# Second row tile's sums by GpSimd's addition, tail inputs third on SyncE's queue, swapped half by copies

## The chip, the cores and the metric

The kernel runs on one core of a Trainium2 chip. The metric is the device time of one execution in microseconds; the time before is the median of three runs. The profile is of one more execution, taken by the hardware profiler; its span runs from the first to the last instruction, and the execution's own time is a little longer than its span.

Engines in the profile: PE is TensorE's matmuls, PEld its weight loads, DVE is VectorE, ACT is ScalarE, POOL is GpSimd, SP is SyncE, which here only issues DMAs. ACTq, SPq and POOLq are the engines' queues.

## The reference

A cross network of six layers on 4096 rows of 416 columns:

```python
B, F, D, L = 4096, 26, 16, 6          # Din = 416
def reference(x0, ws, bs):            # [4096, 416], [6, 416, 416], [6, 416], bf16
    x = x0
    for l in range(ws.shape[0]):
        x = x0 * (x @ ws[l] + bs[l]) + x
    return x
```

Since every layer adds a multiple of x0, x after layer l is x0 * (1 + S_l), where S_l is the sum of all products and biases so far. The kernel keeps S in PSUM, lets TensorE add each layer's product to it, and multiplies by x0 on the way out.

## The kernel before

**Tiling.** The 4096 rows are four blocks of 1024 (s = 0 to 3), each worked through all six layers (l = 0 to 5) before the next. A block is held transposed: features on the partitions, rows on the free axis. The 416 features are three chunks of 128 (c, or m as output and k as input) and a tail of 32. A block has two halves of 512 rows (h). The sum of half h, chunk c lies in PSUM bank 3h+c; banks 6 and 7 (`T_BANK`) hold the tails' sums.

**A layer** has, in this order on TensorE: the main matmuls of the first half (`main`, four 32-column matmuls side by side for each pair of chunks), the tails' contribution to all six banks (`tail_rows`), the tails' own sums (`tail_outs`), and the main matmuls of the second half. As soon as a bank is complete, VectorE adds the bias and multiplies by x0 in one operation of 128x512 (`leave`, L455, or L442 in the last layer but one of the last block): this is the next layer's x. The tail's sum leaves by ScalarE (L465) and GpSimd (L478). The tail exists twice, as it is and with neighbouring groups of 32 partitions swapped; from layer 1 on the swapped half comes from copies of ScalarE and GpSimd (`swap`, L430, L432).

**The head** (s = 0, l = 0). The first 512 rows (`xin_sb`) come in row layout and are transposed by TensorE (L542) and copied by VectorE (L552); the next 512 come by a transposing DMA. `tail_in` (L402) brings the first block's tails into their layout: 16 narrow matmuls against the identity, eight for the straight half into bank 4 and eight for the swapped half into bank 5, copied out by ScalarE (L416) and VectorE (L420). It needs `xtl_sb`, the tail inputs of rows 512 to 1023, which is the third load on ScalarE's queue (L241). In the order of TensorE it stands after the main matmuls of k=1, together with the bias sums, whose result VectorE copies to `cb_sb` (L575).

**The ending** (s = 3). The last layer is computed in row layout, eight row tiles of 128 rows (j = 0 to 7), so that its result goes straight to the output. Row tile j's result gathers in bank `ROW_BANKS[j]` = (6, 7, 0, 1, 2, 3, 4, 5)[j]. The old sums S still lie transposed in banks 0 to 5, so `keep_sum` copies them with the last bias to `sS_sb` (five copies on ScalarE, L488, one on VectorE, L490), and `row_sums` turns them with the identity into the row tiles' banks. TensorE's order: the narrow main matmuls of rows 0 to 3 (`row_main`), the tails of all eight rows (`row_tails`, two groups: rows 0, 2, 4, 6, then rows 1, 3, 5, 7), the sums of rows 1 to 3, then for each of the rows 4 to 7 its main matmuls and sums. VectorE multiplies each finished row by x0 (`finish`, L718), and the row is stored.

Row 0 is treated apart: it has no `row_sums`. Its share of the old sums comes through a transposing DMA of the last layer's x (`transpose_first`, L493, into `xl_sb`), to which GpSimd adds x0 times the last bias (L621, L636). ScalarE copies row 0's new product out of PSUM (L725), GpSimd multiplies (L729) and adds (L733).

**Order.** Each engine runs its instructions in the order in which the code adds them. A small planner (`Plan.add`) works out the waits from keys that each operation reads and writes. For PSUM banks its rule is stricter than for other keys, a reader also waits for the earlier readers on other engines:

```python
            if key[0] == "ps":
                needs += [(r, False) for r in self.readers.get(key, ())]
```

Of the kernel before, what the change touches and what calls it, by code (L numbers as in the profile page):

```python
# [6 lines left out]
FP32 = mybir.dt.float32  # L7
# [111 lines left out]
def bass_standalone__dcn_v2_cross__recsys_kernel(  # L119
# [8 lines left out]
    NC = 3  # L128
# [7 lines left out]
    JS = SB // 128  # L136
    NJ = B // 128
    T_BANK = (6, 7)
    HALVES = range(2)
    CH = range(NC)  # L140

    with ExitStack() as es:

        def sb(name, shape, dt=BF16):
            return es.enter_context(nc.sbuf_tensor(name, shape, dt))
# [15 lines left out]
        f32_sb = sb("f32_sb", [128, D], FP32)  # L161
        xl_sb = sb("xl_sb", [128, DF])
        bl_sb = sb("bl_sb", [128, DF])
        y_sb = sb("y_sb", [128, 2, D], FP32)
        p_sb = sb("p_sb", [128, D], FP32)
        xo_sb = sb("xo_sb", [128, NS - 1, NC, SB])
# [20 lines left out]
        def quad(q):  # L187
            return slice(32 * q, 32 * q + 32)
# [48 lines left out]
        load("scalar", wt_sb[quad(0), 0, :], ws[0, DF:D, :], "wt0", [("wtq",)])  # L237
        for k in CH:
            queue = "sync" if k else "scalar"
            load(queue, w_sb[:, 0, k, :], ws[0, 128 * k:128 * k + 128, :], "w0_%d" % k, [("w", 0, k)])  # L240
        load("scalar", xtl_sb[:, 4:JS, :], x0_v[:, 4:JS, DF:D], "xtl0", [("xtl", 0)])  # L241
        load_transposed(0, H, SB)
# [32 lines left out]
        P.add("gpsimd", lambda e: e.memset(wc_sb[:, :, :], 0.0), writes=[("wc", "wt%d" % i) for i in range(3)])  # L275
        P.add("gpsimd", lambda e: e.memset(y_sb[:, 1, DF:D], 0.0), writes=[("yz",)])

# [123 lines left out]

        def tail_in():  # L402
            def fn(pe):
                for o in range(2):
                    for r in range(2):
                        for g in range(4):
                            j = 2 * (g ^ o) + r
                            src = xin_sb[:, j, DF:D] if j < 4 else xtl_sb[:, j, :]
                            ins = mm(
                                pe, ps[quad(g), TAIL_BANKS[o], r * 128:(r + 1) * 128], src, ident[:, :], r == 0, (0, 32 * g),  # L410
                            )
                return ins

            P.add("tensor", fn, reads=[("ident",), ("xtl", 0), ("xin", 0), ("xin", 1)], adds=[("ps", b) for b in TAIL_BANKS])
            P.add(
                "scalar", lambda e: e.activation(out=x0t_sb[:, 0, 0, :], in_=ps[:, TAIL_BANKS[0], 0:G], func=ACTF.Copy),  # L416
                reads=[("ps", TAIL_BANKS[0])], writes=[("x0t", 0)],
            )
            P.add(
                "vector", lambda e: e.tensor_copy(out=x0t_sb[:, 0, 1, :], in_=ps[:, TAIL_BANKS[1], 0:G]),  # L420
                reads=[("ps", TAIL_BANKS[1])], writes=[("x0t", 0, "swapped")],
            )

        def swap(tile, key, engines):
            for g, eng in enumerate(engines):
                if eng is None:
                    continue
                dst, src = tile[quad(g), 1, :], tile[quad(g ^ 1), 0, :]
                if eng == "scalar":
                    fn = lambda e, d=dst, s=src: e.activation(out=d, in_=s, func=ACTF.Copy)  # L430
                else:
                    fn = lambda e, d=dst, s=src: e.tensor_copy(out=d, in_=s)  # L432
                P.add(eng, fn, reads=[key], parts=[key + ("swapped",)], shifts=True)


# [47 lines left out]

        def keep_sum(h, c, eng):
            lo = 0 if h else 128
            o, i, b = sS_sb[:, c, h * H + lo:(h + 1) * H], ps[:, bank(h, c), lo:H], cb_sb[:, c, L - 1:L]
            if eng == "scalar":
                fn = lambda e: e.activation(out=o, in_=i, func=ACTF.Identity, bias=b)  # L488
            else:
                fn = lambda e: e.tensor_scalar_add(o, i, b)  # L490
            P.add(eng, fn, reads=[("ps", bank(h, c)), ("cb",)], writes=[("sS", c, h)])

        def transpose_first():  # L493
            P.add(
                "sync", lambda e: e.dma_start_transpose(
                    xl_sb.rearrange("p (c f) -> p c f", c=NC), xj[:, 0, :, :].rearrange("p c f -> p (c f)")
                ), reads=[("xT", (L - 1) % 2, c, 0) for c in CH], writes=[("xl",)], dma="xl",
            )
# [34 lines left out]
        B_BANK = 7  # L533
        TAIL_BANKS = (4, 5)

# [47 lines left out]
        for s in range(NS):  # L583
            for l in range(L):
# [3 lines left out]
                if s == 0 and l == 0:  # L588
                    for k in CH:
                        for part in range(2) if k == 0 else (None,):  # L590
                            for m in CH:
                                main(s, l, 0, m, k, part)
                        if k == 1:
                            tail_in()
                            bias_sums()
# [4 lines left out]
                else:  # L600
# [6 lines left out]
                    if ending:  # L607
                        transpose_first()
                    tail_outs(s, l, False)
# [7 lines left out]
                if s > 0 and l == (3 if s < NS - 1 else 2):  # L617
                    store_block(s - 1)
                if s == NS - 1 and l == 3:
                    P.add(  # L620
                        "gpsimd", lambda e: e.tensor_tensor(  # L621
                            out=y_sb[:, 0, 0:DF], in0=xr_sb[:, 0, 0:DF], in1=bl_sb[:, :], op=ALU.mult
                        ), reads=[("xr",), ("bl",)], writes=[("z",)],
                    )
                if ending:
# [8 lines left out]
                    )  # L634
                    P.add(
                        "gpsimd", lambda e: e.tensor_tensor(  # L636
                            out=y_sb[:, 1, 0:DF], in0=y_sb[:, 0, 0:DF], in1=xl_sb[:, :], op=ALU.add
                        ), reads=[("z",), ("xl",)], writes=[("y",)],
                    )
                    for c in CH:  # L640
                        keep_sum(0, c, "scalar")
                for m in CH:
# [3 lines left out]
                if ending:  # L646
                    for c in CH:
                        keep_sum(1, c, ("scalar", "scalar", "vector")[c])
            if s < NS - 1:
# [4 lines left out]
            if s == NS - 2:  # L654
                load("sync", xr_sb[:, :, :], x0_v[:, (NS - 1) * JS:NJ, :], "xr", [("xr",)])
                load("sync", bl_sb[:, :], bs[L - 1:L, 0:DF].to_broadcast([128, DF]), "bl", [("bl",)])

# [56 lines left out]
        def finish(j):  # L714
            b, jj = ROW_BANKS[j], (NS - 1) * JS + j
            if j:
                P.add(
                    "vector", lambda e: e.tensor_tensor(  # L718
                        out=o_sb[:, jj, :], in0=ps[:, b, 0:D], in1=xr_sb[:, j, :], op=ALU.mult
                    ), reads=[("ps", b), ("xr",)], writes=[("ol", j)],  # L720
                )
                return
            t, p, o = f32_sb[:, :], p_sb[:, :], o_sb[:, jj, :]
            P.add(
                "scalar", lambda e: e.activation(out=t, in_=ps[:, b, 0:D], func=ACTF.Copy),  # L725
                reads=[("ps", b)], writes=[("f32",)],
            )
            P.add(
                "gpsimd", lambda e: e.tensor_tensor(out=p, in0=t, in1=xr_sb[:, j, :], op=ALU.mult),  # L729
                reads=[("f32",), ("xr",)], writes=[("p",)],  # L730
            )
            P.add(
                "gpsimd", lambda e: e.tensor_tensor(out=o, in0=p, in1=y_sb[:, 1, :], op=ALU.add),  # L733
                reads=[("p",), ("y",), ("yz",)], writes=[("ol", j)],
            )

        def store_rows(queue, a, b):
            ja = (NS - 1) * JS
            P.add(
                queue, lambda e: e.dma_start(out_v[:, ja + a:ja + b, :], o_sb[:, ja + a:ja + b, :]),  # L740
                reads=[("ol", j) for j in range(a, b)], writes=[("outl", a)], dma="outl",
            )
# [3 lines left out]
        row_tails()  # L746
        finish(0)
        for j in range(1, 4):
            row_sums(j, False)
            finish(j)  # L750
        for j in range(4, 8):
# [3 lines left out]
        P.add("sync", None, reads=[("out", s) for s in range(NS - 1)])  # L755
        STORES = (
            ("scalar", 1, 3), ("scalar", 3, 4), ("sync", 4, 5), ("scalar", 0, 1), ("sync", 5, 6), ("scalar", 6, 7),
            ("sync", 7, 8),
        )
        for queue, a, b in STORES:  # L760
            store_rows(queue, a, b)
        P.add("sync", None, reads=[("outl", a) for _, a, _ in STORES])

# [29 lines left out]
```

## Time and profile before

| what | value |
|---|---|
| median of 3 runs | 127.68 us (127.36 to 127.82) |
| the profiled execution's own time | 128.1 us |
| its span | 126.8 us |
| granted TensorE clock | 1.00 |
| PE busy | 123.6 us, 97% |
| DVE busy | 100.0 us, 79% |
| ACT busy | 43.0 us, 34% |
| POOL busy | 41.0 us, 32% |

By stretches of the span, busy microseconds of each engine:

| stretch, us | PE | DVE | ACT | POOL |
|---|---|---|---|---|
| 0 to 8.7, head | 7.85 | 2.79 | 2.42 | 3.92 |
| 8.7 to 115.4, layers | 106.70 | 88.85 | 36.40 | 32.33 |
| 115.4 to 118.3 | 2.90 | 2.37 | 1.67 | 0.68 |
| 118.3 to 121.0, narrow rows and row tails | 2.70 | 2.33 | 2.00 | 1.66 |
| 121.0 to 125.1, row tiles | 3.47 | 3.67 | 0.47 | 2.37 |
| 125.1 to 126.8, last store | 0 | 0 | 0 | 0 |

A line of the timeline gives the start, the time from the first start to the last end of the group, the engine, the line of the kernel, the operation, what it writes and reads with shapes, the count, and in brackets the engine's idle time before it with what ended it. Groups on PE all bear the line of the helper `mm` (L295); they are told apart by their tiles. Instructions of one engine overlap a little: six of 0.74 us in a row take 4.04 us.

### The profile page before, as it was taken

The numbers are of one execution on the slowest core, as the hardware profiler recorded it, in microseconds if no ns is written. First come the engines' busy times: TensorE is split into PE (matmuls) and PEld (weight loads), VectorE is DVE, ScalarE is ACT, GpSimd is POOL, SyncE is SP. The second block draws the span as 40 slices with busy tenths as digits, with TensorE's granted clock in tenths as the row PEclk, the third lists the DMA queues.
The fourth block names the chain that finished last, engine by engine and source line by source line (L and its number), as shares of the span: only waits on it lengthen the run. The fifth ranks groups of instructions, "written<-read, shape, count | busy, mean of one in ns | idle before, by whom it ended". The sixth has DMA issues, their size and how long they took to land.

```text
span 126.8 us, 5226 instructions
## 1 busy us (share of the span) xinstructions
PE 123.6 (97%) x2373; PEld 64.6 (51%) x2373; DVE 100.0 (79%) x157; ACT 43.0 (34%) x94; POOL 41.0 (32%) x84
## 2 busy tenths in 40 slices
PE   7999999999999999999999999999999999999992
PEld 5654555555545545545545545555555455455561
DVE  2449779779779779788798797797797797797974
ACT  3324225225205225234213242252222252252910
POOL 6505324134014044053122142251320440543590
DMA  3995999010039596107019695107007990070107
GB/s 108 254 253 157 308 158 158 25 25 0 8 83 130 115 213 70 36 16 274 0 32 207 115 163 99 31 16 252 22 0 173 108 292 5 14 255 10 31 20 249
DMA packets 35013, 14.21 MB, mean 112 GB/s; under 512 B 26186, under 2 KB 34992, under 8 KB 34992
## 3 DMA queue, kind: packets, MB, share of 16 engines
q1 hardware_dynamic: 33536, 13.19, 48.4%
q10 hardware_dynamic: 1424, 0.70, 1.9%
q8 instruction: 18, 0.29, 1.0%
q14 instruction: 3, 0.02, 0.1%
q0 software_dynamic: 32, 0.01, 0.0%
HBM read 3.89 MB, written 3.41 MB: 58 GB/s over the span
## 4 chain that ended last, share of the span: by engine, by line
PE 97%; DVE 0%; issue 0%
PE ps L295 94%; PE ps L303 2%; PE ps L542 1%; DVE o_sb L718 0%
## 5 line engine op out<-in xcount | busy, mean ns | idle before, releaser
L455 DVE SCALAR_TENSOR_TENSOR xT_sb<-ps,cb_sb,x0T_sb 128x512 bf16<-128x512 f32 x114 | 76.8, 743 | 15.6 <-PE ps L295 15.6
L295 PE MATMUL ps<-xT_sb,w_sb 128*32 128x512 bf16 (+1 forms) x1596 | 84.2, 364 | 0.0
L295 PEld LDWEIGHTS ps<-xT_sb,w_sb 128*32 128x32 bf16 x1596 | 40.9, 97 | 37.2 <-issue 4.0
L465 ACT ACTIVATE t_sb<-ps,cb_sb 64x256 f32<-64x256 f32 x46 | 21.6, 470 | 57.2 <-PE ps L295 56.9
L478 POOL TENSOR_TENSOR xt_sb<-t_sb,x0t_sb 128x256 bf16<-128x256 f32 x20 | 13.4, 672 | 66.6 <-ACT t_sb L465 66.6
L430 ACT ACTIVATE xt_sb<-xt_sb 32x256 bf16<-32x256 bf16 x38 | 15.7, 414 | 15.1 <-POOL xt_sb L478 14.9
L295 PE MATMUL ps<-x0T_sb,w_sb 128*32 128x512 bf16 (+1 forms) x348 | 19.2, 369 | 0.0
L432 POOL COPY xt_sb<-xt_sb 32x256 bf16<-32x256 bf16 x38 | 14.9, 393 | 2.4
L455 DVE SCALAR_TENSOR_TENSOR xo_sb<-ps,cb_sb,x0T_sb 128x512 bf16<-128x512 f32 x18 | 12.1, 743 | 2.5 <-PE ps L295 2.5
L295 PEld LDWEIGHTS ps<-x0T_sb,w_sb 128*32 128x32 bf16 x348 | 9.1, 101 | 7.7 <-issue 1.1
L295 PE MATMUL ps<-xt_sb,wt_sb 32*128 32x512 bf16 (+1 forms) x152 | 11.6, 326 | 0.0
L295 PE MATMUL ps<-xt_sb,wc_sb 32*128 32x256 bf16 x76 | 7.3, 268 | 0.0
L295 PEld LDWEIGHTS ps<-xt_sb,wt_sb 32*128 32x128 bf16 x152 | 2.3, 91 | 8.1 <-DVE xT_sb L455 8.1
L478 POOL TENSOR_TENSOR xot_sb<-t_sb,x0t_sb 128x256 bf16<-128x256 f32 x3 | 2.0, 672 | 9.9 <-ACT t_sb L465 9.9
L295 PE MATMUL ps<-w_sb,xT_sb 128*32 128x416 bf16 (+1 forms) x60 | 5.0, 339 | 0.0
L442 DVE SCALAR_TENSOR_TENSOR xT_sb<-ps,cb_sb,x0T_sb 128x512 bf16<-128x512 f32 x6 | 4.0, 744 | 0.8 <-PE ps L295 0.8
L718 DVE TENSOR_TENSOR o_sb<-ps,xr_sb 128x416 bf16<-128x416 f32 x7 | 3.7, 583 | 0.8 <-PE ps L295 0.8
L295 PEld LDWEIGHTS ps<-xt_sb,wc_sb 32*128 32x128 bf16 x76 | 3.9, 93 | 0.2
L303 PE MATMUL ps<-const-bfloat16-1.0 128*128 128x256 bf16 x12 | 2.7, 417 | 0.8 <-PEq L778 0.8
L552 DVE COPY x0T_sb<-ps 128x256 bf16<-128x256 bf16 x6 | 1.4, 292 | 2.2 <-PE ps L542 2.2
L295 PEld LDWEIGHTS ps<-w_sb,xT_sb 128*32 128x32 bf16 (+1 forms) x60 | 2.3, 97 | 1.2
L488 ACT ACTIVATE sS_sb<-ps,cb_sb 128x384 bf16<-128x384 f32 (+1 forms) x5 | 2.7, 629 | 0.0
(48 smaller groups left out, 32.3 us busy)
## 6 DMA issues: line engine op xcount, KB each, us to landing
out_dram<-o_sb SPq DMA_DIRECT2D x2, 832.0 KB, 4.8
w_sb<-in_ws_dram SPq DMA_DIRECT2D x5, 312.0 KB, 3.9
out_dram<-o_sb SPq DMA_DIRECT2D x2, 416.0 KB, 3.2
xr_sb<-in_x_dram SPq DMA_DIRECT2D x1, 832.0 KB, 5.0
xin_sb<-in_x_dram SPq DMA_DIRECT2D x2, 208.0 KB, 2.8
wt_sb<-in_ws_dram SPq DMA_DIRECT2D x4, 104.0 KB, 3.3
out_dram<-o_sb ACTq DMA_DIRECT2D x3, 104.0 KB, 1.9
out_dram<-o_sb SPq DMA_DIRECT2D x3, 104.0 KB, 1.7
```

Source lines behind the costliest of these rows:

```text
L295: return pe.matmul(dst, lhsT=lhsT, rhs=rhs, start=start, stop=True, skip_group_check=True, tile_position=pos,)
L303: ins = pe.matmul(ps[:, 7, 0:256], lhsT=const[:, 0:128], rhs=const, start=True, stop=True)
L430: fn = lambda e, d=dst, s=src: e.activation(out=d, in_=s, func=ACTF.Copy)
L432: fn = lambda e, d=dst, s=src: e.tensor_copy(out=d, in_=s)
L442: "vector", lambda e: e.scalar_tensor_tensor(out=xj[:, js, c, :], in0=ps[:, bank(h, c), :].rearrange("p (j f) -> p j f", f=128), scalar=cb ...
L455: "vector", lambda e: e.scalar_tensor_tensor(out=dst, in0=ps[:, bank(h, c), :], scalar=cb_sb[:, c, l:l + 1], in1=x0T_sb[:, c, o:o + H], op ...
L465: "scalar", lambda e, p=p, h=h: e.activation(out=dst[p, :], in_=ps[p, T_BANK[h], 0:G], func=ACTF.Identity, bias=cb_sb[p, NC, l:l + 1]), re ...
L478: "gpsimd", lambda e: e.tensor_tensor(out=dst, in0=t, in1=x0t_sb[:, s, 0, :], op=ALU.mult),
L488: fn = lambda e: e.activation(out=o, in_=i, func=ACTF.Identity, bias=b)
L542: ins = pe.transpose(out=psT[:, b, j * 128:(j + 1) * 128], in_=xin_sb[:, 2 * i + j, c * 128:(c + 1) * 128], identity=ident[:, :],)
L552: "vector", lambda e, d=dst, s=src: e.tensor_copy(out=d, in_=s),
L718: "vector", lambda e: e.tensor_tensor(out=o_sb[:, jj, :], in0=ps[:, b, 0:D], in1=xr_sb[:, j, :], op=ALU.mult), reads=[("ps", b), ("xr",)], ...
```

## The change

Three parts.

*The head.* `xtl_sb` becomes the third load on SyncE's queue; the first layer's weights of k=2 move to ScalarE's queue, and those of k=1 become the fourth load on SyncE's. `tail_in` makes the straight half alone (eight matmuls, bank 5) and stands after the main matmuls of k=0; the swapped half comes from `swap` with VectorE, GpSimd, VectorE and ScalarE.

*The old sums of rows 0 and 1* (JX = 2). VectorE computes (S + last bias) * x0 for 256 rows in the transposed layout (`first_rows_next`, three operations behind the leaves of the first half), and one transposing DMA brings both row tiles to `y_sb` in row layout. Row 1 so loses its `row_sums`, as row 0 had none. The load of the last bias, GpSimd's product and sum with it, and a memset are gone. `keep_sum` leaves out 256 rows in place of 128 in the first half, and all six copies are on ScalarE.

*Finishing.* Row 0's product is split: VectorE the first 128 columns, ScalarE and GpSimd the other 288. Row 1's product is all VectorE's. GpSimd adds y to both (384 columns), ScalarE copies the 32 tail columns of both, and every row has a store of its own.

```diff
-        for k in CH:
-            queue = "sync" if k else "scalar"
+        load("sync", xtl_sb[:, 4:JS, :], x0_v[:, 4:JS, DF:D], "xtl0", [("xtl", 0)])
+        for k, queue in ((0, "scalar"), (2, "scalar"), (1, "sync")):
             load(queue, w_sb[:, 0, k, :], ws[0, 128 * k:128 * k + 128, :], "w0_%d" % k, [("w", 0, k)])
-        load("scalar", xtl_sb[:, 4:JS, :], x0_v[:, 4:JS, DF:D], "xtl0", [("xtl", 0)])
...
+        def tail_in():
+            def fn(pe):
+                for r in range(2):
+                    for g in range(4):
+                        j = 2 * g + r
+                        src = xin_sb[:, j, DF:D] if j < 4 else xtl_sb[:, j, :]
+                        ins = mm(
+                            pe, ps[quad(g), TAIL_BANK, r * 128:(r + 1) * 128], src, ident[:, :], r == 0, (0, 32 * g),
+                        )
+                return ins
+
+            P.add("tensor", fn, reads=[("ident",), ("xtl", 0), ("xin", 0), ("xin", 1)], adds=[("ps", TAIL_BANK)])
+            P.add(
+                "scalar", lambda e: e.activation(out=x0t_sb[:, 0, 0, :], in_=ps[:, TAIL_BANK, 0:G], func=ACTF.Copy),
+                reads=[("ps", TAIL_BANK)], writes=[("x0t", 0)],
+            )
+            swap(x0t_sb[:, 0], ("x0t", 0), ("vector", "gpsimd", "vector", "scalar"))
...
-        def keep_sum(h, c, eng):
-            lo = 0 if h else 128
+        def keep_sum(h, c):
+            lo = 0 if h else JX * 128
             o, i, b = sS_sb[:, c, h * H + lo:(h + 1) * H], ps[:, bank(h, c), lo:H], cb_sb[:, c, L - 1:L]
-            if eng == "scalar":
-                fn = lambda e: e.activation(out=o, in_=i, func=ACTF.Identity, bias=b)
-            else:
-                fn = lambda e: e.tensor_scalar_add(o, i, b)
-            P.add(eng, fn, reads=[("ps", bank(h, c)), ("cb",)], writes=[("sS", c, h)])
-
-        def transpose_first():
+            P.add(
+                "scalar", lambda e: e.activation(out=o, in_=i, func=ACTF.Identity, bias=b),
+                reads=[("ps", bank(h, c)), ("cb",)], writes=[("sS", c, h)],
+            )
+
+        def first_rows_next():
+            o = (NS - 1) * SB
+            for c in CH:
+                P.add(
+                    "vector", lambda e, c=c: e.scalar_tensor_tensor(
+                        out=yT_sb[:, :, c, :], in0=ps[:, bank(0, c), 0:JX * 128].rearrange("p (j f) -> p j f", f=128),
+                        scalar=cb_sb[:, c, L - 1:L],
+                        in1=x0T_sb[:, c, o:o + JX * 128].rearrange("p (j f) -> p j f", f=128),
+                        op0=ALU.add, op1=ALU.mult,
+                    ), reads=[("ps", bank(0, c)), ("cb",), ("x0T", NS - 1, c, 0)], writes=[("yT", c)],
+                )
             P.add(
                 "sync", lambda e: e.dma_start_transpose(
-                    xl_sb.rearrange("p (c f) -> p c f", c=NC), xj[:, 0, :, :].rearrange("p c f -> p (c f)")
-                ), reads=[("xT", (L - 1) % 2, c, 0) for c in CH], writes=[("xl",)], dma="xl",
+                    y_sb.rearrange("p j (c f) -> p (j c) f", f=128), yT_sb.rearrange("p j c f -> p (j c f)")
+                ), reads=[("yT", c) for c in CH], writes=[("y",)], dma="y",
             )
...
                                 main(s, l, 0, m, k, part)
+                        if k == 0:
+                            tail_in()
                         if k == 1:
-                            tail_in()
                             bias_sums()
...
                     if ending:
-                        transpose_first()
+                        first_rows_next()
...
-                        keep_sum(0, c, "scalar")
+                        keep_sum(0, c)
...
-                        keep_sum(1, c, ("scalar", "scalar", "vector")[c])
+                        keep_sum(1, c)
...
+            p, y, hi = p_sb[:, j, :], y_sb[:, j, 0:DF], D if j else 128
+            P.add(
+                "vector", lambda e: e.tensor_tensor(out=p[:, 0:hi], in0=ps[:, b, 0:hi], in1=xr[:, 0:hi], op=ALU.mult),
+                reads=[("ps", b), ("xr",)], writes=[("p", j, "vector")],
+            )
+            if hi < D:
+                P.add(
+                    "scalar", lambda e: e.activation(out=f32_sb[:, hi:D], in_=ps[:, b, hi:D], func=ACTF.Copy),
+                    reads=[("ps", b)], writes=[("f32",)],
+                )
+                P.add(
+                    "gpsimd", lambda e: e.tensor_tensor(out=p[:, hi:D], in0=f32_sb[:, hi:D], in1=xr[:, hi:D], op=ALU.mult),
+                    reads=[("f32",), ("xr",)], writes=[("p", j, "gpsimd")],
+                )
+            P.add(
+                "gpsimd", lambda e: e.tensor_tensor(out=o[:, 0:DF], in0=p[:, 0:DF], in1=y, op=ALU.add),
+                reads=[("p", j, "vector"), ("p", j, "gpsimd"), ("y",)], writes=[("ol", j)],
+            )
...
         row_tails()
-        finish(0)
-        for j in range(1, 4):
+        for j in range(JX):
+            finish(j)
+        for j in reversed(range(JX)):
+            finish_tail(j)
+        for j in range(JX, 4):
             row_sums(j, False)
             finish(j)
...
-        STORES = (
-            ("scalar", 1, 3), ("scalar", 3, 4), ("sync", 4, 5), ("scalar", 0, 1), ("sync", 5, 6), ("scalar", 6, 7),
-            ("sync", 7, 8),
-        )
...
+        for queue, j in (
+            ("scalar", 2), ("sync", 3), ("scalar", 0), ("sync", 4), ("scalar", 5), ("sync", 6), ("scalar", 1), ("sync", 7),
+        ):
+            store_row(queue, j)
```

More of the change, by code (lines that the diff above doesn't have):

```diff
@@ L137, in bass_standalone__dcn_v2_cross__recsys_kernel @@
     NJ = B // 128
+    JX = 2
     T_BANK = (6, 7)
@@ L161, in bass_standalone__dcn_v2_cross__recsys_kernel @@
         f32_sb = sb("f32_sb", [128, D], FP32)
[L162 to L165, printed above, removed]
+        yT_sb = sb("yT_sb", [128, JX, NC, 128])
+        y_sb = sb("y_sb", [128, JX, DF])
+        p_sb = sb("p_sb", [128, JX, D], FP32)
         xo_sb = sb("xo_sb", [128, NS - 1, NC, SB])
@@ L275, in bass_standalone__dcn_v2_cross__recsys_kernel @@
         P.add("gpsimd", lambda e: e.memset(wc_sb[:, :, :], 0.0), writes=[("wc", "wt%d" % i) for i in range(3)])
-        P.add("gpsimd", lambda e: e.memset(y_sb[:, 1, DF:D], 0.0), writes=[("yz",)])
         def replicate():
@@ L400, in tail_outs @@
             )
[L402 to L410, printed above, removed]
-                            )
[L412 to L422, printed above, removed]
         def swap(tile, key, engines):
@@ L533, in bass_standalone__dcn_v2_cross__recsys_kernel @@
         B_BANK = 7
-        TAIL_BANKS = (4, 5)
+        TAIL_BANK = 5
         def turn_rows(i):
@@ L618, in bass_standalone__dcn_v2_cross__recsys_kernel @@
                     store_block(s - 1)
[L619 to L624, printed above, removed]
                 if ending:
@@ L634, in bass_standalone__dcn_v2_cross__recsys_kernel @@
                     )
[L635 to L639, printed above, removed]
                     for c in CH:
-                        keep_sum(0, c, "scalar")
+                        keep_sum(0, c)
                 for m in CH:
@@ L655, in bass_standalone__dcn_v2_cross__recsys_kernel @@
                 load("sync", xr_sb[:, :, :], x0_v[:, (NS - 1) * JS:NJ, :], "xr", [("xr",)])
-                load("sync", bl_sb[:, :], bs[L - 1:L, 0:DF].to_broadcast([128, DF]), "bl", [("bl",)])
         s, l = NS - 1, L - 1
@@ L714, in finish @@
         def finish(j):
-            b, jj = ROW_BANKS[j], (NS - 1) * JS + j
-            if j:
+            b, o, xr = ROW_BANKS[j], o_sb[:, (NS - 1) * JS + j, :], xr_sb[:, j, :]
+            if j >= JX:
                 P.add(
-                    "vector", lambda e: e.tensor_tensor(
-                        out=o_sb[:, jj, :], in0=ps[:, b, 0:D], in1=xr_sb[:, j, :], op=ALU.mult
-                    ), reads=[("ps", b), ("xr",)], writes=[("ol", j)],
+                    "vector", lambda e: e.tensor_tensor(out=o, in0=ps[:, b, 0:D], in1=xr, op=ALU.mult),
+                    reads=[("ps", b), ("xr",)], writes=[("ol", j)],
@@ L721, in finish @@
                 )
                 return
-            t, p, o = f32_sb[:, :], p_sb[:, :], o_sb[:, jj, :]
+            p, y, hi = p_sb[:, j, :], y_sb[:, j, 0:DF], D if j else 128
             P.add(
-                "scalar", lambda e: e.activation(out=t, in_=ps[:, b, 0:D], func=ACTF.Copy),
-                reads=[("ps", b)], writes=[("f32",)],
-            )
+                "vector", lambda e: e.tensor_tensor(out=p[:, 0:hi], in0=ps[:, b, 0:hi], in1=xr[:, 0:hi], op=ALU.mult),
+                reads=[("ps", b), ("xr",)], writes=[("p", j, "vector")],
+            )
@@ L728, in finish @@
+            if hi < D:
[7 more added lines that the diff above has]
+                )
             P.add(
-                "gpsimd", lambda e: e.tensor_tensor(out=p, in0=t, in1=xr_sb[:, j, :], op=ALU.mult),
@@ L730, in finish, with finish_tail @@
-                reads=[("f32",), ("xr",)], writes=[("p",)],
+                "gpsimd", lambda e: e.tensor_tensor(out=o[:, 0:DF], in0=p[:, 0:DF], in1=y, op=ALU.add),
+                reads=[("p", j, "vector"), ("p", j, "gpsimd"), ("y",)], writes=[("ol", j)],
             )
+        def finish_tail(j):
             P.add(
-                "gpsimd", lambda e: e.tensor_tensor(out=o, in0=p, in1=y_sb[:, 1, :], op=ALU.add),
-                reads=[("p",), ("y",), ("yz",)], writes=[("ol", j)],
-            )
@@ L737, in store_rows, with store_row @@
-        def store_rows(queue, a, b):
-            ja = (NS - 1) * JS
+                "scalar", lambda e: e.activation(
+                    out=o_sb[:, (NS - 1) * JS + j, DF:D], in_=p_sb[:, j, DF:D], func=ACTF.Copy
+                ), reads=[("p", j, "vector" if j else "gpsimd")], writes=[("olt", j)],
+            )
+        def store_row(queue, j):
+            jj = (NS - 1) * JS + j
             P.add(
-                queue, lambda e: e.dma_start(out_v[:, ja + a:ja + b, :], o_sb[:, ja + a:ja + b, :]),
-                reads=[("ol", j) for j in range(a, b)], writes=[("outl", a)], dma="outl",
+                queue, lambda e: e.dma_start(out_v[:, jj, :], o_sb[:, jj, :]),
+                reads=[("ol", j)] + ([("olt", j)] if j < JX else []), writes=[("outl", j)], dma="outl",
@@ L755, in bass_standalone__dcn_v2_cross__recsys_kernel @@
         P.add("sync", None, reads=[("out", s) for s in range(NS - 1)])
-        STORES = (
-            ("scalar", 1, 3), ("scalar", 3, 4), ("sync", 4, 5), ("scalar", 0, 1), ("sync", 5, 6), ("scalar", 6, 7),
-            ("sync", 7, 8),
[L759 to L762, printed above, removed]
+        for queue, j in (
+            ("scalar", 2), ("sync", 3), ("scalar", 0), ("sync", 4), ("scalar", 5), ("sync", 6), ("scalar", 1), ("sync", 7),
+        ):
+            store_row(queue, j)
+        P.add("sync", None, reads=[("outl", j) for j in range(JS)])
         P.emit(nc, es)
```

## The prediction

> **What bounds the kernel now.** I read the chain of waits first, then the timeline of the last 15 us, of the head, and of 0.8 us before the row tails.
>
> ```profile
> PE 97%; DVE 0%; issue 0%
> PE ps L295 94%; PE ps L303 2%; PE ps L542 1%; DVE o_sb L718 0%
> ```
>
> TensorE is the chain from start to end, so a microsecond moves the end only if it is put on TensorE or makes it wait. Next the head, then the ending:
>
> ```profile
> 7.07 0.22 PE L295 MATMUL ps<-ident,xin_sb 128*32 128x128 bf16 x2
> 7.24 0.22 PE L295 MATMUL ps<-ident,xtl_sb 128*32 128x128 bf16 x2
> 7.52 0.39 ACT L416 ACTIVATE x0t_sb<-ps 128x256 bf16<-128x256 f32 x1 [3.25 <-PE ps L295]
> 7.52 0.42 DVE L420 CAST x0t_sb<-ps 128x256 bf16<-128x256 f32 x1 [2.13 <-PE ps L295]
> 7.86 0.17 DVE L575 COPY cb_sb<-ps 128x24 f32<-128x24 f32 x1
> 8.14 0.60 PE L295 MATMUL ps<-x0t_sb,wt_sb 32*128 32x512 bf16 x7
> ...
> 115.93 4.04 DVE L442 SCALAR_TENSOR_TENSOR xT_sb<-ps,cb_sb,x0T_sb 128x512 bf16<-128x512 f32 x6 [0.83 <-PE ps L295]
> 117.57 2.68 ACT L488 ACTIVATE sS_sb<-ps,cb_sb 128x384 bf16<-128x384 f32 x5
> 118.03 1.20 SPq L495 DMA_TRANSPOSE xl_sb<-xT_sb  x1
> 119.89 0.74 DVE L490 TENSOR_SCALAR sS_sb<-ps,cb_sb 128x512 bf16<-128x512 f32 x1
> 120.51 0.35 PE L295 MATMUL ps<-wt_sb,xt_sb 32*128 32x416 bf16 x4
> 120.73 0.34 PE L295 MATMUL ps<-wt_sb,xt_sb 32*128 32x416 bf16 x4
> 121.02 0.68 PE L295 MATMUL ps<-ident,sS_sb 128*128 128x128 bf16 x9
> 121.40 3.71 DVE L718 TENSOR_TENSOR o_sb<-ps,xr_sb 128x416 bf16<-128x416 f32 x7 [0.76 <-PE ps L295]
> 121.53 0.69 PE L295 MATMUL ps<-w_sb,xT_sb 128*128 128x416 bf16 x3
> ```
>
> ```profile
> 119.23 0.74 DVE L442 SCALAR_TENSOR_TENSOR xT_sb<-ps,cb_sb,x0T_sb 128x512 bf16<-128x512 f32 x1
> 119.55 0.71 ACT L488 ACTIVATE sS_sb<-ps,cb_sb 128x512 bf16<-128x512 f32 x1
> ```
>
> The reader is to see that VectorE has no gap from 115.93 to 120.63: six leaves (start to start (4.04-0.74)/5 = 0.66) and the last sums' copy (L490). The second row-tail group (120.73) overwrites banks 7, 1, 3 and 5; bank 5 is the one that L490 reads until 120.63. TensorE comes 0.1 us after it. That is all the slack there is.
>
> **The change, part by part** (times on the old clock).
>
> *Head.* Of 16 narrow transposes 8 go: 7.07 to 7.24 is three steps for 12 of them, 0.056 each, so four steps become two: -0.11. They now run behind the k=0 matmuls, at about 6.25, and need the tail inputs by then. Those landed at 1.72+4.3 = 6.0 as third on ScalarE's queue; as third on SyncE's, behind 2 x 208 KB of rows (landing after 2.8), I expect about 5. SyncE still issues four loads ahead of its transposing load; w0_1, now fourth, and w0_2, now ScalarE's third, are 104 KB each (landing after 3.1 to 3.4: by 5.6) and needed from 6.5 and 7.3. VectorE's 0.42 cast goes; the swapped half comes behind the ScalarE copy: transposes done near 6.7, copy 0.39, then copies of 32x256 (ScalarE 0.41, GpSimd 0.39 by L430 and L432, two on VectorE below 0.42 in all) to about 7.6. The tails would start at 8.03, so 0.4 us of cover hides this; without it the step would cost the difference. The cb copy stays early enough, as the bias matmuls stay behind k=1. Head: -0.11.
>
> *Off the path.* GpSimd loses a memset (0.14), the product L621 (0.92) and the sum L636 (0.91), SyncE a 96 KB load. GpSimd waits for ScalarE 66.6 us over the run: worth nothing.
>
> *Three new VectorE operations* (first_rows_next) stand on VectorE between the leaves of the first and of the second half, where it has no gap. None of this shape is in the trace. Below: the 128x256 cast steps in 0.34 (7.52 to 7.86): 1.03 for three. Above: no cheaper than the 512-wide leave, 3 x 0.66 = 1.98. Between, at about 1 ns a column (128x416 0.58 less 128x256 0.42 over 160): 0.66-0.26 = 0.40, so **1.2**; I take this, as operation and operands are the leave's. The last leave ends at 119.98+1.2 = 121.18. Rows 4 to 7 need these leaves only from 121.5: no cost there. The transposing DMA starts after 119.2 in place of 118.03, with twice the columns: 2.3 to 4.6 us (the old one; the x0T load), so y is there at 121.5 to 123.8.
>
> *The copies of the sums* are now all ScalarE's. Each waits for the bank's VectorE readers before it, so the second half's follow the late leaves: the last starts 0.06 (ScalarE to GpSimd takes 117.55 to 117.62) after 121.18 and lasts 0.71: 121.95, where L490 ended at 120.63. On ScalarE the copy of row 0's product queues behind it (120.95 becomes about 121.9), and GpSimd waits for that. **The second row tails start near 122.01 in place of 120.73: +1.28** on TensorE, with everything behind them; the first ones (bank 4) at about 121.35.
>
> *Row 1's sums* leave TensorE: three of the 128-wide matmuls at 0.056: -0.17.
>
> *Finishing.* VectorE takes a narrow row 0 (128 columns, about 0.3) and rows 1 to 7 at 0.50 steps (3.71-0.58 less the last wait): row 1 from 122.4, row 7 could start at 125.4, and TensorE gives row 7 at 124.5+1.28-0.17 = 125.6: hidden by 0.2. GpSimd: product of 288 columns (0.97 x 288/416 = 0.68) from 122.3, two sums of 384 (1.06 x 384/416 = 0.98 each) to about 125.0, then ScalarE's store (0.4, landing 1.9): 127.0, against 127.9 for row 7's. Two ScalarE copies of 32 columns wait for nothing late. Stores: eight single rows, four on each queue; row 6's issue (0.37) is over before row 7 is ready.
>
> **Sum:** 1.28-0.17-0.11 = **+1.0 us**: the span goes from 126.8 to 127.8. The profiled execution took 128.1 us as a whole, 1.3 around the span; the median of the runs is 127.68. The 1.0 on the median: **128.7 us**, +0.8%. With the lower price of the three operations 128.5, with the upper 129.5. What a measurement of this kernel tells from no change is about 0.5%, 0.64 us.
>
> The Trainium skill, TensorE: Matmul & The Clock Gate, section What's actually happening, has the array at half its rate until some 3.4 us of activity, and again after an idle window of that length. The trace agrees on the head (256 columns step by 0.21 at 5.6, 512 by 0.22 at 6.9), though the granted clock reads 1.00 throughout; with the new idle stretches, 0.8 and 0.5 us, the rule would leave the sum as it is.
>
> **The rivals.**
>
> *B, not slower: ScalarE's copies don't follow VectorE's leaves.* Place: the banks of the row tails. If ScalarE reads its banks as TensorE finishes them (118.3), its six copies end near 120.6, and the row tails keep their time: decided at 120.67, the end of the last copy from which TensorE waits. Then only -0.28 is left: 127.4, within 0.5%. For it: before, no copy is seen to wait for VectorE; ScalarE was simply busy. Against: the plan adds that wait for every second reader of a bank, and the copies of before start at 118.98 and 119.55, each after its leave.
> The Trainium skill, PSUM — Partial Sum Buffer, section PSUM bank collisions raise a hardware error, counts two engines' reads of one bank as a collision; no run here shows one, and by it B's overlap would not be allowed.
>
> *C, GpSimd's chain sets the end.* If y lands at 123.8, the sums end at 125.8 and row 1's store at 127.7, 0.2 before row 7's; with a GpSimd sum 30% dearer, it is 0.4 behind: 129.1. For it: these two sums have no shape in the trace. Against: 0.9 us of room by the nearest rows.
>
> *D, the head waits.* Tail inputs later than 6.25, or a swapped half later than 8.03, are paid one for one. By the old landing on the old queue (6.0) there is no cost; at 0.4 late 129.1.
>
> *E, TensorE falls to its head rate after the idle stretch.* Rows 4 to 7 step by 0.70 (121.53 to 122.22); twice that is +2.8: 131.5. Against: nothing in the trace slows after the head.
>
> **How the numbers follow.** Forecast 0.68 (own range 128.35 to 129.0), B 0.14, C 0.07, D 0.08, E 0.03. The predicted time is 128.7; the range 128.0 to 129.2 takes in C and D and leaves out B, E and the forecast's edge, some 0.2. Slower by over 0.5% (above 128.32): 0.62 of the forecast, C, D and E: 0.79. B gives 0.10 for no change and 0.04 for faster; with the rest of the forecast: same 0.16, faster 0.05.
>
> **What would show it.** The second row-tail matmuls about 1.2 us later against the row matmuls that end ahead of them; three 128x256 VectorE operations between the leaves, with 0.4 from start to start; the last ScalarE copy ending just before the row tails; head tails at about 8.03. Wrong, if the row tails follow the row matmuls at 0.1 us as before, or if the end hangs on GpSimd's store.

## The result, and the profile after

The changed kernel takes 129.09 us (median of 6 runs, 128.83 to 129.28) against 127.50 for the kernel before on the same chip (6 runs, 127.17 to 127.82): a ratio of 1.0126, 95% interval 1.0106 to 1.0147. It is slower by 1.6 us. Its profiled execution took 129.1 us with a span of 127.8; against the profile shown of before (126.8) that is only +1.0. The missing 0.6 us are explained below: the profiled execution of before, with 128.1 us, was one of its longest.

The chain of waits after, by line:

```profile
PE 93%; DVE 3%; ACT 1%; issue 1%; ACTq 0%
PE ps L293 89%; DVE xT_sb L436 2%; PE ps L301 2%; ACT sS_sb L482 1%; PE ps L545 1%; DVE yT_sb L490 1%; DVE o_sb L710 0%; ACTq L109 0%
```

TensorE no longer is the whole chain: VectorE's leaves (L436), the three new operations (L490) and ScalarE's copies of sums (L482) have come into it. The timeline of the ending shows where, first a line of before, then the kernel after:

```profile
115.47 0.60 PE L295 MATMUL ps<-xt_sb,wt_sb 32*128 32x512 bf16 x7
```

```profile
115.26 0.60 PE L293 MATMUL ps<-xt_sb,wt_sb 32*128 32x512 bf16 x7
...
115.73 2.07 DVE L436 SCALAR_TENSOR_TENSOR xT_sb<-ps,cb_sb,x0T_sb 128x512 bf16<-128x512 f32 x3 [0.84 <-PE ps L293]
...
117.71 1.26 DVE L490 SCALAR_TENSOR_TENSOR yT_sb<-ps,cb_sb,x0T_sb 128x256 bf16<-128x256 f32 x3
...
118.22 1.26 ACT L482 ACTIVATE sS_sb<-ps,cb_sb 128x256 bf16<-128x256 f32 x3 [0.88 <-DVE yT_sb L490]
118.89 2.06 DVE L436 SCALAR_TENSOR_TENSOR xT_sb<-ps,cb_sb,x0T_sb 128x512 bf16<-128x512 f32 x3
...
119.73 2.00 ACT L482 ACTIVATE sS_sb<-ps,cb_sb 128x512 bf16<-128x512 f32 x3 [0.25 <-DVE xT_sb L436]
...
121.17 0.36 PE L293 MATMUL ps<-wt_sb,xt_sb 32*128 32x416 bf16 x4 [0.79 <-DVE xT_sb L436]
...
121.87 0.36 PE L293 MATMUL ps<-wt_sb,xt_sb 32*128 32x416 bf16 x4 [0.33 <-ACT sS_sb L482]
...
122.17 0.51 PE L293 MATMUL ps<-ident,sS_sb 128*128 128x128 bf16 x6
...
122.82 3.27 DVE L710 TENSOR_TENSOR o_sb<-ps,xr_sb 128x416 bf16<-128x416 f32 x6
...
123.29 1.78 POOL L729 TENSOR_TENSOR o_sb<-p_sb,y_sb 128x384 bf16<-128x384 f32 x2
```

The three operations stand between the two groups of leaves, from 117.71 to 118.89: 1.18 us. Each ScalarE copy starts 0.03 to 0.10 us after the end of the VectorE operation on its bank. TensorE stands idle for 0.79 us ahead of the first row tails and for 0.33 us ahead of the second. For the first wait the profile names the last leave (ended 120.94); the first row tails also overwrite bank 4, which ScalarE's last copy but one reads until 121.07, 0.10 us ahead of them, so it is as likely this copy. Six sum matmuls in place of nine follow. From the start of the last layer's first tail rows (115.26; before 115.47) to TensorE's end it is now 10.20 us; before it was 9.01. This stretch is called the ending below; the head is the stretch from the span's start to the first layer's first tail rows.

The head, from the timeline of its first 13 us:

```profile
1.72 0.43 SPq L195 DMA_DIRECT2D xtl_sb<-in_x_dram  x1
2.19 0.50 SPq L195 DMA_DIRECT2D w_sb<-in_ws_dram  x1
...
5.01 1.03 PE L293 MATMUL ps<-x0T_sb,w_sb 128*32 128x256 bf16 x24
...
6.02 0.10 PEld L293 LDWEIGHTS ps<-ident,xin_sb 128*32 128x32 bf16 x2 [0.27 <-DMA xtl_sb<-in_x_dram]
...
6.09 0.22 PE L293 MATMUL ps<-ident,xtl_sb 128*32 128x128 bf16 x2
...
6.43 0.83 PE L293 MATMUL ps<-x0T_sb,w_sb 128*32 128x512 bf16 x12
...
6.78 0.57 DVE L408 COPY x0t_sb<-x0t_sb 32x256 bf16<-32x256 bf16 x2 [1.38 <-ACT x0t_sb L424]
...
7.94 0.60 PE L293 MATMUL ps<-x0t_sb,wt_sb 32*128 32x512 bf16 x7
```

and the loads of the weights of k=1 and of the tail inputs with their time from issue to landing (count, size of one, median us), first before, then after:

```profile
w_sb<-in_ws_dram SPq DMA_DIRECT2D x1, 104.0 KB, 3.1
xtl_sb<-in_x_dram ACTq DMA_DIRECT2D x1, 32.0 KB, 4.3
```

```profile
w_sb<-in_ws_dram SPq DMA_DIRECT2D x1, 104.0 KB, 4.1
xtl_sb<-in_x_dram SPq DMA_DIRECT2D x1, 32.0 KB, 4.3
```

On SyncE's queue the tail inputs land no earlier than they did on ScalarE's: 1.72+4.3 = 6.0 both times. The weights of k=1, now behind them, land at 2.19+4.1 = 6.3 in place of 1.71+3.1 = 4.8. TensorE waits for the tail inputs at 6.02, and, by the landing, between 6.15 and 6.43 for the weights of k=1. The profile itself gives this second gap to nothing; that it is this wait is read from the times, k=1 starting 0.14 us after the landing at 6.29.

### The profile page after: what moved, and what is told of

The parts are those of the page before. It is cut to its first block, busy times and chain, and to the rows that moved or that the text cites. A ratio compares the mean times of both kernels' runs of the same rounds, so it can differ in the third digit from the quotient of the medians.

```text
span 127.8 us, 5218 instructions
## 1 busy us (share of the span) xinstructions
PE 123.4 (97%) x2362; PEld 64.1 (50%) x2362; DVE 101.1 (79%) x161; ACT 44.2 (35%) x98; POOL 39.8 (31%) x83
## 4 chain that ended last, share of the span: by engine, by line
PE 93%; DVE 3%; ACT 1%; issue 1%; ACTq 0%
PE ps L293 89%; DVE xT_sb L436 2%; PE ps L301 2%; ACT sS_sb L482 1%; PE ps L545 1%; DVE yT_sb L490 1%; DVE o_sb L710 0%; ACTq L109 0%
## 5 line engine op out<-in xcount | busy, mean ns | idle before, releaser
L436 DVE SCALAR_TENSOR_TENSOR xT_sb<-ps,cb_sb,x0T_sb 128x512 bf16<-128x512 f32 x6 | 4.1, 744 | 0.8 <-PE ps L293 0.8
L482 ACT ACTIVATE sS_sb<-ps,cb_sb 128x256 bf16<-128x256 f32 (+1 forms) x6 | 3.3, 580 | 1.1 <-DVE yT_sb L490 0.9
L710 DVE TENSOR_TENSOR o_sb<-ps,xr_sb 128x416 bf16<-128x416 f32 x6 | 3.2, 582 | 0.1
```

The costliest lines, as they stand in the source:

```text
L436: "vector", lambda e: e.scalar_tensor_tensor(out=xj[:, js, c, :], in0=ps[:, bank(h, c), :].rearrange("p (j f) -> p j f", f=128), scalar=cb ...
L482: "scalar", lambda e: e.activation(out=o, in_=i, func=ACTF.Identity, bias=b),
L710: "vector", lambda e: e.tensor_tensor(out=o, in0=ps[:, b, 0:D], in1=xr, op=ALU.mult),
```

## The experiments

Theory A, formed on these two traces: the ending costs 1.2 us, the late loads cost the head some 0.4 more, and the profile of before hides the latter by being a late execution. Its rival, theory B, is the prediction's reckoning: the head gains 0.1 to 0.2 us, and all of the 1.6 is the ending's.

### The two halves of the change apart

`e1_head_only` is the kernel before with the change's head, `e2_end_only` the kernel before with its ending.

> The kernel before with the head of the changed one alone (load order, tail_in after k=0, copies for the swapped half). Theory A: the weights of k=1 land at 6.0 to 6.3 in place of 4.8, TensorE waits for them wherever it reaches full rate early; the runs are 0.2 to 0.45 us slower than before, and the profile shows a gap of TensorE ahead of the k=1 matmuls. Theory B (as predicted): the head saves 0.1 to 0.2 us, and all of the 1.6 us is the ending's.

> The kernel before with the ending of the changed one alone. Theory A: +1.1 to +1.25 us, second row tails about 1.45 us after the last narrow row matmuls' start in place of 0.5. Theory B: +1.6 us or more. Both: ScalarE's last copy is what the second row tails wait for.

The times are medians; the ratios with their intervals are reckoned from all runs and differ a little from the medians' quotient. e1: 127.86 us against 127.24, ratio 1.0042 (1.0024 to 1.0060). e2: 128.69, ratio 1.0110 (1.0083 to 1.0137). Both halves cost, as theory A has it; B's gain in the head does not exist. In e1's profile the last transposes start at 5.96 and the k=1 matmuls only at 6.32, 0.14 us after their weights landed at 6.18; the ending is 9.01:

```profile
5.96 0.22 PE L294 MATMUL ps<-ident,xtl_sb 128*32 128x128 bf16 x2
6.32 0.83 PE L294 MATMUL ps<-x0T_sb,w_sb 128*32 128x512 bf16 x12
```

In e2's profile the ending is 10.20 as in the changed kernel. Both sizes came out above theory A's: e1 by 0.62 (interval 0.31 to 0.76 us) for 0.2 to 0.45, e2 by 1.45 (1.06 to 1.74) for 1.1 to 1.25. The runs of e2 alone can't tell 1.2 from theory B's 1.6; e1 and the ending of e2's profile do. Added, the halves come to 1.9 to 2.1 us, more than the 1.6 of the whole; the intervals allow for it.

### The ending, term by term

These kernels start from e2. `e3_end_no_ops` and `e5_end_no_ops_late` leave out the three operations and zero their tile (so two row tiles lack their old sums), e3 in the head, e5 in layer 3 of the last block:

```diff
-            for c in CH:
-                P.add(
-                    "vector", lambda e, c=c: e.scalar_tensor_tensor(
...
+        P.add("gpsimd", lambda e: e.memset(yT_sb[:, :, :, :], 0.0), writes=[("yT", c) for c in CH])
```

`e4_end_keep_vec` puts the last copy of sums back on VectorE:

```diff
-                        keep_sum(1, c)
+                        keep_sum(1, c, ("scalar", "scalar", "vector")[c])
```

> As the ending alone, but the three VectorE operations are left out, and the tile that they fill is zeroed by GpSimd at the start; rows 0 and 1 of the last block lack their old sums. If the operations' place on VectorE is the cause: the row tails come back to about 0.1 us behind the row matmuls (0.07 later than before, as the last copy is on ScalarE), and the time is 0.05 to 0.2 us below the kernel before (three matmuls fewer). Rival, that ScalarE's last copy or GpSimd's chain costs the time: still 0.5 us or more above the kernel before.

> As the ending alone, but the last of the six copies of sums goes back to VectorE, as it was before. If the delay is that of VectorE's three operations: 0.1 us below the ending alone, still about 1.0 to 1.1 us above the kernel before. If the move of this copy to ScalarE is the cause: 0.5 us or more below the ending alone.

> As e3, but the tile is zeroed by GpSimd in the last block, so that the head is that of the kernel before; rows 0 and 1 of the last block lack their old sums. If the three operations are the ending's whole cost: from the last layer's tail rows to TensorE's end 9.0 us as before (against 10.2), and the time within 0.2 us of the kernel before; e3's 0.5 us were its head. If the ending holds another cost: again 0.4 us or more above the kernel before.

e3: 127.80 against 127.24, 1.0038 (1.0019 to 1.0056). By the runs alone this is the rival's number. But its profile has an ending of 9.03, so what the runs have on top must lie ahead of it. e5, with the memset moved out of the head, has the same ending, 9.03, and the time of the kernel before: 127.60 against 127.46, ratio 1.0004 (0.9976 to 1.0033). That the memset in the head costs e3 anything is not shown: the two intervals overlap, and the head of e3's profile, 7.71, lies among those of the kernel before (below). e4: 128.39 against 127.24, 1.0090 (1.0063 to 1.0116), ending 9.99; by its profile the last copy is worth 0.21, between the two expectations and nearer the first.

The timeline of e5, with ScalarE's six copies and the two groups of row tails:

```profile
117.23 3.19 ACT L486 ACTIVATE sS_sb<-ps,cb_sb 128x256 bf16<-128x256 f32 x6
...
120.18 0.35 PE L294 MATMUL ps<-wt_sb,xt_sb 32*128 32x416 bf16 x4
...
120.56 0.36 PE L294 MATMUL ps<-wt_sb,xt_sb 32*128 32x416 bf16 x4
```

and of e4, with the copies and the second row tails' weight load:

```profile
119.22 1.34 ACT L486 ACTIVATE sS_sb<-ps,cb_sb 128x512 bf16<-128x512 f32 x2 [0.25 <-DVE xT_sb L440]
120.35 0.74 DVE L488 TENSOR_SCALAR sS_sb<-ps,cb_sb 128x512 bf16<-128x512 f32 x1
...
121.15 0.10 PEld L294 LDWEIGHTS ps<-wt_sb,xt_sb 32*128 32x128 bf16 x4 [0.37 <-DVE sS_sb L488]
```

Without the operations ScalarE runs its six copies without a break, until 120.42, and the second row tails follow the first by 0.38; in the kernel before it was 0.22. With the last copy back on VectorE, the row tails wait for VectorE. So the ending's terms are: three operations 10.202-9.025 = 1.18; the last copy on ScalarE 10.20-9.99 = 0.21; row 1's sums gone, -0.17 (three matmuls at 0.056; no run takes them alone). Their sum is 1.22, and 10.201-9.005 = 1.20 was measured. That a copy of ScalarE waits for the leave of its bank is the planner's rule for PSUM banks; no run leaves this wait out, and none puts the three operations behind the second half's leaves, so how much of the 1.18 another order would save is not known.

### The head, load order and copies apart

`e6_loads_only` is the kernel before with the new load order alone, `e7_copies_only` the kernel before with the new tail_in, its place and its copies alone. First e6, then e7:

```diff
+        load("sync", xtl_sb[:, 4:JS, :], x0_v[:, 4:JS, DF:D], "xtl0", [("xtl", 0)])
+        for k, queue in ((0, "scalar"), (2, "scalar"), (1, "sync")):
...
-        load("scalar", xtl_sb[:, 4:JS, :], x0_v[:, 4:JS, DF:D], "xtl0", [("xtl", 0)])
```

```diff
+                        if k == 0:
+                            tail_in()
                         if k == 1:
-                            tail_in()
                             bias_sums()
```

> The kernel before with the changed order of the first loads alone; the 16 transposes stay behind k=1. Theory A, that the late weights of k=1 hold the head: k=1 starts at 6.2 to 6.4 and the first layer's tail rows at 8.0 to 8.1 however early TensorE reaches full rate; 0.5 to 0.8 us above the kernel before. Rival, that the chain of copies for the swapped half holds it: no slower than before.

> The kernel before with its own loads, but tail_in after k=0, with eight transposes and the copies. Theory A: the weights of k=1 are there at 4.9, but TensorE now waits ahead of k=1 for the tail inputs, which land at 6.0: tail rows at about 7.7 to 7.8, 0.2 to 0.5 us above the kernel before. Rival, that the load order is the whole cost: 0.1 us below the kernel before.

e6: 128.10 against 127.46, 1.0041 (1.0020 to 1.0062). e7: 127.79, 1.0029 (1.0006 to 1.0052). Each costs by itself, and the two together (e1) cost no more than e6 alone, as one expects where the last landing decides. e6 waited longer than theory A said: its weights of k=1 landed at 6.63, k=1 started at 6.76 in place of 6.2 to 6.4, and the tail rows at 8.50 in place of 8.0 to 8.1. Its timeline names the wait:

```profile
4.88 0.84 PE L294 MATMUL ps<-x0T_sb,w_sb 128*32 128x256 bf16 x24
6.76 0.83 PE L294 MATMUL ps<-x0T_sb,w_sb 128*32 128x512 bf16 x12 [1.04 <-DMA w_sb<-in_ws_dram]
...
8.50 0.39 PE L294 MATMUL ps<-x0t_sb,wt_sb 32*128 32x512 bf16 x4
```

and that of e7 the other (weight loads):

```profile
5.00 0.56 PEld L295 LDWEIGHTS ps<-x0T_sb,w_sb 128*32 128x32 bf16 x24
6.05 0.10 PEld L295 LDWEIGHTS ps<-ident,xin_sb 128*32 128x32 bf16 x2 [0.50 <-DMA xtl_sb<-in_x_dram]
```

In e6 TensorE has done k=0 by 5.7 and waits 1.04 us for the weights of k=1. In e7 these are there, and it waits for the tail inputs instead. Either way the transfer that lands last sets the end of the head: from the landing of the weights of k=1 to the first tail rows it is 1.65 us both in the changed kernel (6.29 to 7.94) and in e1 (6.18 to 7.83). The copies (done at 7.4 in e7, tail rows at 7.69) hold nothing up.

### Two heads with earlier tail inputs

Both have e7's tail_in and SyncE's queue as before; on ScalarE's queue `e8_xtl_first` issues the tail inputs, the weights of k=0 and the tails' weights, `e11_xtl_second` the tails' weights, the tail inputs and the weights of k=0. The edit of e8:

```diff
+        load("scalar", xtl_sb[:, 4:JS, :], x0_v[:, 4:JS, DF:D], "xtl0", [("xtl", 0)])
+        for k in CH:
...
+        load("scalar", wt_sb[quad(0), 0, :], ws[0, DF:D, :], "wt0", [("wtq",)])
```

> As e7, with the tail inputs as the first load on ScalarE's queue, then the weights of k=0, and the tails' weights last. Theory A: the tail inputs land by 5.5, TensorE waits for nothing ahead of k=1, tail rows at 7.0 to 7.4: 0 to 0.15 us below the kernel before. If the chain of copies holds the head: tail rows at 7.6 or later, 0.2 us or more above.

> As e8, but the tails' weights stay first on ScalarE's queue, the tail inputs second, the weights of k=0 third. Theory A, that the head is whatever lands last: tail inputs by 4.6, the weights of k=0 at 4.8 to 5.2, tail rows at 7.1 to 7.4, 0 to 0.2 us below the kernel before. If something else than the landings holds the copies' head: tail rows at 7.6 or later.

Neither met theory A's times; the tail rows came at the rivals' 7.6 or later. e8: 127.99 against 127.46, 1.0028 (1.0004 to 1.0051), tail rows at 8.03; the lines are of its timeline. The tail inputs did land early (issue to landing 2.8), but the tails' weights, now last, took 4.1; their copies to the other partitions began at 5.98 to 6.09, GpSimd was busy with them until 7.47, and its part of the swapped half came only at 7.53:

```profile
6.09 1.11 POOL L284 COPY wt_sb<-wt_sb 32x416 bf16<-32x416 bf16 x2 [2.32 <-DMA wt_sb<-in_ws_dram]
...
7.53 0.39 POOL L410 COPY x0t_sb<-x0t_sb 32x256 bf16<-32x256 bf16 x1
...
8.03 0.59 PE L295 MATMUL ps<-x0t_sb,wt_sb 32*128 32x512 bf16 x7 [0.55 <-POOL x0t_sb L410]
```

e11: 128.22 against 127.79, 1.0076 (1.0033 to 1.0119). Here the weights of k=0 are last on that queue, and k=0 starts at 5.80 behind a wait of 0.76 for them. Four of its runs lie at 129.7 to 130.3, and one far above; why, no profile shows. The other seven lie at 127.9 to 128.3. In both kernels the tail inputs landed as early as expected, and the load put at the end of ScalarE's queue decided: in e11 it landed at 5.67 in place of 4.8 to 5.2, and in e8 theory A had not counted GpSimd's copies that wait for it. No order tried beats that of the kernel before.

### The kernel before, twice more

> The kernel before, once more, for its profile. Theory A says that its span varies with the moment at which TensorE's steps in the head fall from 0.21 to 0.11 us, and that the profile shown of before was a late one: the tail rows of the first layer start anywhere from 7.1 to 8.2, and what follows them has the same length to 0.05 us. Rival: the head is the same in every execution (8.1), and the runs differ elsewhere.

> As e9, a further execution of the kernel before, with the same two expectations: tail rows anywhere from 7.1 to 8.2 by theory A, at 8.1 by the rival.

One execution each of the unchanged code: 127.20 us (span 125.9) and 127.81 (126.5). Timeline of the first:

```profile
4.84 1.49 PE L295 MATMUL ps<-x0T_sb,w_sb 128*32 128x256 bf16 x36
...
7.23 0.60 PE L295 MATMUL ps<-x0t_sb,wt_sb 32*128 32x512 bf16 x7
```

and of the second:

```profile
5.12 1.78 PE L295 MATMUL ps<-x0T_sb,w_sb 128*32 128x256 bf16 x36
...
7.81 0.40 PE L295 MATMUL ps<-x0t_sb,wt_sb 32*128 32x512 bf16 x6
```

and, for comparison, of the profile shown of before:

```profile
4.99 2.25 PE L295 MATMUL ps<-x0T_sb,w_sb 128*32 128x256 bf16 x36
```

The same 36 matmuls of k=0 and k=1 take 1.49, 1.78 and 2.25 us. The first layer's tail rows start at 7.23, 7.81 and 8.14. What follows is the same in all 13 profiles of this case: 107.32 us from there to the last layer's tail rows, and 2.35 to 2.38 from TensorE's end to the span's. So a span is the head, plus 107.32, plus the ending, plus 2.36, and only two of these vary:

| kernel | head, us | ending, us | span, us |
|---|---|---|---|
| before, as shown | 8.14 | 9.01 | 126.8 |
| before, e9 | 7.23 | 9.01 | 125.9 |
| before, e10 | 7.81 | 9.01 | 126.5 |
| changed | 7.94 | 10.20 | 127.8 |
| e1, head only | 7.83 | 9.01 | 126.5 |
| e2, ending only | 7.60 | 10.20 | 127.5 |

Theory A holds: the profile of before was late by up to 0.9 us. The 17 runs of the kernel before made beside e9 and e10, on one chip, agree: their spans go from 125.8 to 127.0. The median of 127.50 goes with a span of 126.2 (the runs are 1.3 longer than their spans), so with a head of about 7.5; the changed kernel's 129.09 with one of 7.9. That is 0.4 in the head and 1.2 in the ending: the 1.6 measured.

## Why the prediction was right, and where it was not

**The bound and the mechanism** were right: the second row tails wait for ScalarE's last copy, this for the last leave, and this for three operations put where VectorE had no gap. The operations took 1.18 us (1.2 forecast; 0.39 from start to start), the row tails moved by 121.87-115.26 less 120.73-115.47 = 1.35 us (1.28), and row 1's sums gave back 0.17. The ending came to +1.20 in place of 1.28-0.17 = 1.11. The 0.1 is in the hand-overs: from the last leave (ended 120.94) to ScalarE's copy 0.10 in place of 0.06, and from the copy's end (121.72) to the row tails 0.15 in place of 0.06.

**Finishing** was hidden, as forecast: y landed 2.8 us after 119.00, GpSimd's sums took 0.91 each (0.98) and ended at 125.07, ahead of VectorE's last row, which TensorE released.

**The head is the step that failed.** The prediction put it at -0.11, from tail inputs landing at "about 5" and the weights of k=1 "by 5.6". They landed at 6.0 and 6.3, and the head came to about +0.4. For the tail inputs no row stood behind "about 5". For the weights of k=1, which became the fourth load of SyncE's queue, it took 3.4, the median of the third and the fourth load of before; the third alone took 3.1, so the fourth 3.7, which already gives 2.19+3.7 = 5.9. The eight matmuls saved are real, but what decides is the last landing. Rival D had such a wait, with the chance of 0.08 and as a case of its own, but by its own mark (tail inputs later than 6.25) the landing at 6.0 would have cost nothing, and it did not name the weights.

**The sum's base** hid this. The sum was made against the one profile shown, in which k=0 ended at 6.25, after the tail inputs had landed. In the six other profiles with that head it ended at 5.5 to 6.1, and with the changed order a transfer that lands at 6.0 or 6.3 is waited for. The prediction saw the slow steps of that profile's head and took their length for fixed. It counted the 0.21 at 5.6 as agreeing with the rule it cites; TensorE had been at work since 0.83, for 4.8 us, so this row spoke against it, and for a late head.

**The number** was helped by luck. The shift was 1.6 us in place of 1.0, but the median of before, 127.68 in the sum, was 127.50 in the comparison, which hid 0.18 of the difference. 129.09 is above the forecast's own range (to 129.0) and inside the stated one only because that was widened for C and D. (A slip without effect: 0.62, C, D and E add up to 0.80, not 0.79.)

**Rival B** (ScalarE's copies free of VectorE's leaves) fell: its mark, row tails 0.1 us behind the row matmuls, is not there, and the waits name VectorE and ScalarE. **C** (GpSimd's chain) and **E** (TensorE at half rate after the idle stretch) did not show: rows 4 to 7 still step by 0.70 (122.52 to 123.22).

## What to carry to other kernels

Before an operation is moved to an engine with idle time, look for idle time at that place: VectorE is idle for a fifth of the span, and has none in the 4.7 us that the three operations went into, where they cost 1.18 us to save 0.17. A load that is moved ahead of others delays what it passes, and may itself land no earlier; here the transfer that landed last set the head. One profile is one execution: where its span lies in the spread of the runs should be settled before small terms are summed on it.

## What the runs showed of the hardware

TensorE's steps fall from 0.21 to 0.11 us for 256 columns, and from 0.11 to 0.06 for 128, at a moment that varies between executions of the same code: between 4.1 and 4.4 us in e9, at 5.8 in e10, at 6.6 in the profile of before, with a granted clock of 1.00 in all. In e8 the transposes step by 0.06 from 3.5 us on. This is worth up to 0.9 us of the span. The Trainium skill, TensorE: Matmul & The Clock Gate, section What's actually happening, says that the window that opens the clock gate runs freely and doesn't start with the kernel, and gives the moment half a microsecond to either side. In these traces the moment does vary, but over 2.2 us for the kernel before; the window itself no run shows.

A load of 512 pieces of 64 bytes (32 KB) took 4.0 to 4.6 us to land as the third on a queue, on either queue, 3.0 as the second (e11) and 2.8 as the first (e8). The 104 KB of weights of k=1 took 4.0 to 4.4 us as the fourth load of SyncE's queue, behind the tail inputs, in place of 3.1 to 3.8 as the third in the kernels whose loads are those of before. As the fourth load of before, the weights of k=2 took 3.7 to 4.0 behind 104 KB, so a good part of this is the place in the queue. Not all is its own queue's order: in e8, with SyncE's queue as before, the weights of k=1 took 4.1.
